# Storing the rows of each load in another order in DRAM: a decode attention and gated feed-forward kernel on one core

## The chip, the core and the metric

The kernel runs on one core of a Trainium2 chip. The metric is the device time of one execution in microseconds (us); the median of several runs is used. Beside the times there is one profiled execution, whose page and trace are read below.

## What is computed

One token is decoded for a batch of two (B = 2, D = 512). The input is normalised, and the result is the input plus an attention branch plus a feed-forward branch, all in float32. The attention has 32 heads of width 128, each with its own keys and values, and looks only at the last W = 2048 of 8192 cached positions.

```
W = min(4096, max(256, Sk // 4))              # 2048
q = (x @ wq) ... (B, Hq, Sq, Dh)
k = k_cache[:, :, Sk - W:, :]
v = v_cache[:, :, Sk - W:, :]
scores = einsum("bhqd,bhkd->bhqk", q, k) * Dh ** -0.5
o = einsum("bhqk,bhkd->bhqd", softmax(scores), v)
A = o ... @ wo
B = ((x w_gate) * (x w_up)) @ w_down          # F = 1376
out = x + A(layernorm(x)) + B(layernorm(x))
```

The caches and weights that must be read once come to 159.48 MB, and each byte is used for very little arithmetic.

## The kernel before

**One stream.** The host packs everything that the kernel reads in bulk into one flat array, `stream`, in the order of use (`laid_out`, from L495). `blocks` (L41) lists the pieces: a small first piece (normalisation input, selection matrices and the first head's weights), then steps that hold in turn keys (`k`), query weights (`wq`), values (`v`), output weights (`wo`), the feed-forward weights (`wg`, `wu`, `wd`). A piece is a block of 128 rows; row p holds what goes to SBUF partition p, and all rows of a block have one length. A full step has 13,824 floats (55,296 bytes) a row, 6,912 KB in all; 16 of the 29 stream loads are of this size. The last, shorter loads split the end of the stream, so that work on the last head can start early. One more array, `wd_rest`, holds the last 96 rows of `w_down` and is loaded as 96 rows of 512 floats, after the last stream load.

**Loads.** `pump` (L138) issues the loads from SyncE's queue (SP), one `dma_start` for each block. Full steps live in a pool `steps` of three buffers (`BUFS = 3`, L119). When a buffer's last field has been used, `done` (L164) frees it and calls `pump`, so the next load is queued behind those that are running. Nothing else issues bulk loads. A load's rows are source rows of equal length that lie one behind the other:

```
src = stream[at : at + P * (c1 - c0)].rearrange("(p i) -> p i", p=P)
sp.dma_start(tiles[key][:, c0:c1], src)
```

Both sides of this load count 128 rows, the partition being the outermost count. The hardware deals the rows of each load to 16 DMA engines.

**Compute.** For each head VectorE multiplies the keys with the broadcast query (`products`) and adds up over the head width (`sums`), GpSimd finds the maximum and the sum over the partitions, ScalarE takes the exponential (`weights`), and TensorE weighs the values (`weigh`), brings the result into place (`transpose`) and adds the output projection to one accumulator (`project_o`). The values of a head come three heads after its keys (`LAG = 3`). The class `InOrder` keeps every engine's instructions in the order in which the code writes them; since its one line L92 makes the calls, nearly all instructions stand under L92 in the profile, and groups are told apart by their tiles (`step`, `q`, `s`, `o_ps`, `acc`).

## Time and profile before

| what | value |
|---|---|
| median of 3 runs | 378.63 us (378.44 to 378.70) |
| the profiled execution's own time | 379.42 us |
| its span, first to last instruction | 377.6 us |
| read from DRAM | 159.48 MB, 422 GB/s over the span |
| busy: TensorE, VectorE, ScalarE, GpSimd | 258.7, 293.7, 58.5, 25.4 us |
| packets of the load queue, share of 16 engines | 98.2% |
| granted TensorE clock, mean | 0.783 |
| a 6,912 KB load, issue to landing, median | 33.8 us |

The span is what the page's shares refer to; the rest of the execution's time lies around it. "DMA share" is the mean busy share of the 16 DMA engines in a stretch, and GB/s is what they moved. The time from issue to landing contains the wait behind loads that are already queued. The trace also holds a record of each DMA packet, with queue, start, duration and size, but not the engine that moved it.

### The profile page before, as it was taken

To read this page: it belongs to the slowest core of one execution; us is meant where nothing else is said; L and a number is where in the kernel's file an instruction comes from. 1 tells how busy PE (TensorE), PEld (TensorE's weight loads), DVE (VectorE), ACT (ScalarE), POOL (GpSimd) and SP (SyncE) were. 2 spreads that over 40 slices of the span, in tenths; PEclk is the share of its full clock that TensorE was granted. 3 is DMA by queue.
4 is the path that set the end of the run, shared out by engine and by line. 5 is a ranking of instruction groups with operands and counts; after the bars stand their busy time and mean duration, and the time that the engine had idled before them with its cause. 6 is when DMAs were issued, how large, how long until landed. Compare 5 with 4: busy or idle time off the path is not lost.

```text
span 377.6 us, 2826 instructions
## 1 busy us (share of the span) xinstructions
PE 258.7 (69%) x1070; PEld 87.9 (23%) x1070; DVE 293.7 (78%) x144; ACT 58.5 (15%) x256; POOL 25.4 (7%) x78
## 2 busy tenths in 40 slices
PE   3386597986548586766858476585756769537995
PEld 3241122231112222212212121231211222111343
DVE  3299691998599499769949977994996799599940
ACT  1011001122011120202112020121202011211131
POOL 1001000000000001000000000000000000000010
PEclk9996968888697666868858696885968677855999
DMA  8999999899999999999999999999999999999994
GB/s 326 461 434 455 439 394 469 387 457 453 400 451 451 398 457 404 441 457 404 452 439 406 457 404 445 451 412 440 445 398 463 418 417 434 446 435 418 416 416 162
DMA packets 4328, 159.65 MB, mean 423 GB/s; under 512 B 492, under 2 KB 508, under 8 KB 988
## 3 DMA queue, kind: packets, MB, share of 16 engines
q1 hardware_dynamic: 4316, 159.48, 98.2%
q8 instruction: 8, 0.13, 0.1%
q14 instruction: 4, 0.03, 0.0%
HBM read 159.48 MB, written 0.00 MB: 422 GB/s over the span
## 4 chain that ended last, share of the span: by engine, by line
DMA 68%; PE 15%; DVE 14%; ACT 1%; SPq 1%; issue 1%; DVEq 0%
DMA step<-in_stream_dram 68%; DVE s L92 7%; DVE step L92 7%; PE o_ps L92 6%; PE q L92 4%; PE acc L92 3%; PE tr L92 1%; SPq L92 1%; ACT o_sb L92 0%; ACT oT L92 0%; DVE o_sb L92 0%; DVE m L92 0%; ACT hT L92 0%; DVE o_out L92 0%; DVE rec L92 0%
## 5 line engine op out<-in xcount | busy, mean ns | idle before, releaser
L92 DVE TENSOR_TENSOR step<-step,q 128x4096 f32<-128x4096 f32 x31 | 136.6, 4407 | 53.0 <-DMA step<-in_stream_dram 53.0
L92 PE MATMUL q<-step,xnb 128*128 128x512 f32 (+1 forms) x128 | 94.1, 886 | 74.5 <-DMA step<-in_stream_dram 74.5
L92 DVE TENSOR_REDUCE s<-step 128x32 f32<-128x4096 f32 x32 | 141.4, 4420 | 1.1
L92 PE MATMUL o_ps<-step,p 128*16 128x512 f32 x512 | 71.3, 695 | 10.6 <-DMA step<-in_stream_dram 10.6
L92 PEld LDWEIGHTS q<-step,xnb 128*128 128x128 f32 x128 | 32.9, 280 | 131.4 <-DMA step<-in_stream_dram 75.9
L92 PE MATMUL acc<-step,oT 128*17 128x512 f32 (+1 forms) x88 | 37.2, 578 | 9.3 <-ACT oT L92 8.1
L92 ACT COPY o_sb<-o_ps 128x512 f32<-128x512 f32 x24 | 14.0, 585 | 145.9 <-PE o_ps L92 145.9
L92 PE MATMUL tr<-first,o_sb 128*128 128x2 f32 (+2 forms) x192 | 26.3, 257 | 14.9 <-ACT o_sb L92 13.3
L92 PEld LDWEIGHTS tr<-first,o_sb 128*128 128x128 f32 x192 | 24.5, 196 | 36.5 <-ACT o_sb L92 33.0
L290 POOL PARTITION_ALL_REDUCE mm<-m x32 | 11.3, 355 | 286.2 <-DVE rec L92 179.9
L92 PEld LDWEIGHTS o_ps<-step,p 128*16 128x16 f32 x512 | 13.8, 107 | 70.6 <-issue 56.9
L92 ACT ACTIVATE nm<-mm 128x2 f32<-128x2 f32 x32 | 6.5, 203 | 130.2 <-POOL mm L290 130.2
L92 ACT ACTIVATE p<-s,nm 128x16 f32<-128x16 f32 x64 | 19.2, 300 | 1.0
L92 ACT ACTIVATE oT<-tr,rec 128x1 f32<-128x1 f32 x64 | 12.2, 260 | 27.1 <-PE tr L92 27.1
L306 POOL PARTITION_ALL_REDUCE sum<-rs x32 | 12.7, 398 | 53.4 <-ACT p L92 53.4
L92 PE MATMUL o_ps<-step,xn 128*2 128x512 f32 (+1 forms) x48 | 13.5, 597 | 0.0
L92 DVE TENSOR_TENSOR step<-step,tr 128x4096 f32<-128x4096 f32 x1 | 4.4, 4422 | 9.8 <-DMA step<-in_stream_dram 9.8
L92 ACT ACTIVATION_READ_ACCUMULATOR p<-s,nm 128x1 f32 x64 | 12.0, 187 | 0.0
L92 PEld LDWEIGHTS acc<-step,oT 128*17 128x17 f32 x88 | 4.9, 98 | 19.6 <-ACT oT L92 11.9
L92 PE MATMUL acc<-step,hT 128*17 128x128 f32 (+2 forms) x58 | 8.0, 361 | 0.7 <-DMA step<-in_stream_dram 0.7
L92 PE MATMUL q<-xnb,mean_w 128*128 128x512 f32 (+1 forms) x16 | 7.8, 581 | 0.0
L92 DVE TENSOR_TENSOR o_out<-acc,x_nat 128x128 f32<-128x128 f32 x1 | 0.3, 292 | 9.1 <-PE acc L92 9.1
(35 smaller groups left out, 38.5 us busy)
## 6 DMA issues: line engine op xcount, KB each, us to landing
step<-in_stream_dram SPq DMA_DIRECT2D x16, 6912.0 KB, 33.8
step<-in_stream_dram SPq DMA_DIRECT2D x2, 6400.0 KB, 32.9
step<-in_stream_dram SPq DMA_DIRECT2D x1, 6784.0 KB, 46.0
step<-in_stream_dram SPq DMA_DIRECT2D x1, 6656.0 KB, 29.2
step<-in_stream_dram SPq DMA_DIRECT2D x1, 5376.0 KB, 15.7
step<-in_stream_dram SPq DMA_DIRECT2D x1, 4864.0 KB
step<-in_stream_dram SPq DMA_DIRECT2D x2, 2304.0 KB, 17.2
step<-in_stream_dram SPq DMA_DIRECT2D x1, 1280.0 KB, 14.1
```

The costliest lines, as they stand in the source:

```text
L92: made = call(*args, **kwargs)
L290: nc.gpsimd.partition_all_reduce(mm, m, P, bass_isa.ReduceOp.max)
L306: nc.gpsimd.partition_all_reduce(sum_t[h], rs, P, bass_isa.ReduceOp.add)
```

## The change

The rows of each stream block are stored in another order. With the 128 rows numbered 8 q + n (q from 0 to 15, n from 0 to 7), row 8 q + n now lies at place 16 n + q of its block. The host stores it so, and the load's source pattern undoes it: it counts 16 (q), then 8 (n), then the row's floats. The source's outermost step is one stored row, its second step 16 stored rows. The destination is the same tile as before and gets the same row in each partition. All 29 stream loads are changed in this way, the small first one included; `wd_rest`, `x_rows` and the output are not. The order of instructions on each engine stays.

```diff
@@ -26,6 +26,8 @@
 FH = [(0, 2 * FB), (2 * FB, F)]
 LAG = 3
 RB = 16
+NQ = 16
+NR = P // NQ
 M = RB * (B - 1) + 1
@@ -158,7 +160,9 @@
             if at is None:
                 sp.dma_start(tiles[key][:FR, c0:c1], wd_rest)
             else:
-                src = stream[at : at + P * (c1 - c0)].rearrange("(p i) -> p i", p=P)
+
+                src = stream[at : at + P * (c1 - c0)]
+                src = src.rearrange("(n q i) -> q n i", n=NR, q=NQ)
                 sp.dma_start(tiles[key][:, c0:c1], src)
@@ -540,9 +544,10 @@
     parts = [
-        np.concatenate([field(kind, i) for kind, i, _ in fields], axis=1).ravel()
+        np.concatenate([field(kind, i) for kind, i, _ in fields], axis=1)
         for _, fields in blocks()
     ]
+    parts = [a.reshape(NQ, NR, -1).swapaxes(0, 1).ravel() for a in parts]
```

## The prediction

> **What bounds the kernel now.** I read the page from the top: engine shares, then the 40 slices, the queues, the chain, and last the windows of the trace and its packet records.

> ```profile
> PE 258.7 (69%) x1070; PEld 87.9 (23%) x1070; DVE 293.7 (78%) x144; ACT 58.5 (15%) x256; POOL 25.4 (7%) x78
> ...
> DMA  8999999899999999999999999999999999999994
> ...
> q1 hardware_dynamic: 4316, 159.48, 98.2%
> ...
> DMA 68%; PE 15%; DVE 14%; ACT 1%; SPq 1%; issue 1%; DVEq 0%
> ```

> No compute engine is full: VectorE, the busiest, works 78% of the span. The DMA digits are 9 nearly throughout, and the packets of queue q1 fill 98.2% of the time of 16 engines. The chain puts 68% on transfers into `step`; its PE and DVE pieces are work done between two landings while the next load is already running. So the length of the kernel is the length of the stream, and what matters is how fast each of the 16 engines gets through its rows.

> The windows (columns: stretch, busy time of PE, PEld, DVE, ACT, POOL, clock, DMA share, GB/s) show the steady rate and the tail:

> ```profile
> 20.00:60.00 40.00, 29.02 (x81) 9.25 (x79) 33.67 (x16) 4.88 (x19) 2.61 (x7) 0.83 1.00 434
> 110.00:160.00 50.00, 34.16 (x130) 10.34 (x130) 42.41 (x20) 8.07 (x38) 3.71 (x10) 0.73 1.01 437
> ...
> 371.00:372.00 1.00, 0.93 (x8) 0.93 (x8) 0.00 (x0) 0.02 (x1) 0.00 (x0) 1.00 0.65 195
> ```

> In the steady part a full DMA share moves 434 to 437 GB/s. In the tail, from 371 to 372 us, a share of 0.65 moves 195 GB/s, which is 300 GB/s per full share. The packet records say why. One packet is one row of a load, as many packets of a size as the load has rows (2048 of 55,296 bytes for 16 loads of 128 rows). In the steady part a row never varies: 2,041 ns shortest, 2,044 median, 2,049 at the ninth tenth; the 11 rows over 2,070 ns each cover the time of an instruction-load packet of q8 or q14. In the tail they vary. The last load but one has 128 rows of 4,096 bytes: 159 ns at best, but up to 287 once the rows of `wd_rest` (96 rows of 2,048 bytes) have begun beside them; those take 84 ns alone and up to 176 in that stretch (one 232). A row that takes 176 instead of 84 ns has met another that wanted the same thing at the same moment. Short fixed costs explain only part: 2,048 bytes in 84 ns on 16 engines would still be 390 GB/s.

> So two facts: rows of 128-row loads run together without touching each other, and rows of the one load that is cut up differently (96 rows, six to an engine) slow others, and are slowed, to about double.

> **The change, part by part.** *Instructions.* No compute instruction, wait, buffer or byte changes. The same 29 stream issues stand at the same places of SP's queue, the same 128 rows of the same sizes go to the same partitions, and the number of packets stays. Costs at nothing: the host's reordering is outside the measured time. An issue with one more source dimension lasts between the 0.39 us of the first load and the 0.73 us of the `x_nat` issue in the SP timeline; only the first one is uncovered, so 0 to 0.3 us. I take 0: all later ones lie beside a running load.

> *Places in DRAM.* At any moment the 16 engines read other addresses. What can that give? At most what rows now lose against their shortest time, since a row cannot be said to be read-bound when 2048 of them agree within some 0.4%. Adding packets by size, the 29 stream loads take 369.8 us per engine as measured and 367.9 at the shortest of each size: a gain of at most 1.9 us, 0.3 of which is instruction loading. The loss to be had: none that a row shows.

> [...]

> *The cut among engines.* This is the part that decides. Before, source and destination both count 128 rows, outermost. After, the source counts 16, then 8, then the row; the destination still counts 128. The engines cannot be dealt the rows by one count of 128 on both sides any more. The natural cut is by the 16: engine q gets piece q, that is rows 8 q to 8 q + 7, written to eight neighbouring partitions. The trace doesn't say which engine carries which row before, but if it were that cut already, nothing would change here; if it is another, every stream load becomes what only `wd_rest` is now: a load cut into runs of neighbouring partitions. Bounds for a row of such a load: 1.0 times its time (as the rows of 128-row loads) and 2.1 times (176 over 84). The nearest row is that of `wd_rest`, because it is the only load of this trace that isn't counted by 128 on both sides, and the slowed rows appear exactly with it. I take 2: two engines want one place and each gets half of it.

> [...]

> Would two engines that start together stay together? While they share, both run at half; when the one ahead moves on, both run at full until the other follows. Both always run at one rate, so a lead is kept and neither grows nor shrinks. The first rows of 16 engines begin within about 0.15 us, so a lead is about 0.1 us. It is saved once per change of place. I take two changes per load (a choice), so 2 x 29 x 0.1 = 5.8 us. All 16 engines must end a load before its semaphore is full, and three buffers let a luckier pair run ahead by two loads at most, so the pair with the smallest lead sets the time.

> *Sum.* Packets of queue q1 take 370.7 us per engine; the profiled execution took 379.42, so 8.8 us is start, gaps, the work after the last landing and what lies around the span; it stays. Stream rows at their shortest, 367.9, doubled: 735.7. The 96-row load, `x_nat` and semaphore packets: 0.9. 735.7 + 0.9 + 8.8 - 5.8 = 739.6, say 740. The profiled execution lies 0.2% over the 378.63 median of the runs, less than the rounding here. What hid the transfers' neighbours stays hidden: VectorE's 293.7 us fit into 740, and a step's buffer is free (1.5 heads a load, each 4.4 us of products and 4.4 of sums, are 13 us of VectorE work) long before the next 33 us load has landed, so SP's waits end earlier, not later.

> **Rivals.** *Leads grow.* If one of two sharing engines gets 51% of the place, its lead grows by 4% of what is still shared at each of 58 stays; the shared part shrinks by 0.96 each time, and 22.7 of 58 stays are shared in sum: 367.9 x 0.39 = 144 us more, 523. At 50.5% it is 34.5 stays and 598. [...] Against: the slowed 4,096-byte rows (1.8 times) and 2,048-byte rows (2.1 times) of the tail suffer alike.

> *The change doesn't alter the cut, or the place isn't shared.* Then only addresses move, and the time is that of before, 378.6. For it: the trace shows no engine numbers, and the tail's slow rows could come from mixing two sizes. Against: 6,144- and 8,192-byte rows follow each other in the queue the same way, and their ninth tenths lie within 4% of their shortest.

> *Faster, by the read side alone.* Cut unchanged, and neighbouring reads end the loss at the start, where 43,008-byte rows take 1,650 ns on average against 1,587, and the small ones everywhere. Worth the 1.6 us that isn't instruction loading: 377.0. It decides only where the place is not shared at all, since one shared row costs more than it can save. Against: nearly all rows already stand at their shortest.

> **How the numbers follow.** About 0.2% is what a measurement of this kernel can tell from no change. Full sharing, 700 to 765 (low end: leads of 0.7 us; high end: without leads the sum is 745, with 2.1 for 2 it is 782, and 765 is about half-way): 68%. Growing leads, 400 to 700: 20%. Addresses alone with no effect: 6%; faster by the read side: 3%; slightly slower (start or issue): 3%. The forecast is 740. The range of 490 to 765 holds nearly all of the first case and two thirds of the second, some 80%. Faster 0.03, same 0.06, slower 0.91.

> **What would show it.** Right: 55,296-byte rows near 4.1 us instead of 2.04, the slices near 217 GB/s with a DMA share still 9 in every slice, landings of the 6,912 KB loads about double, VectorE's share near 40%, and the chain with far more than 68% on DMA. Growing leads would show in slices that climb from 217 towards 434 GB/s over the span. Wrong: rows still at 2,041 to 2,049 ns. Then the cut is unchanged or two engines don't disturb each other, and the step "the nearest row is that of `wd_rest`" has failed.

## The result and the profile after

The changed kernel takes 770.78 us, the median of 6 runs (765.96 to 774.64); the kernel before took 378.71 us beside it. The ratio is 2.0345, with a 95% interval of 2.0303 to 2.0388. The way and the mechanism were forecast; the time lies 4% over the 740 us of the forecast and 0.8% over the upper end of its range, 765 us. The profiled execution took 765.96 us, the shortest of the six, with a span of 764.2 us.

From the page of the changed kernel: the engines' busy shares, the slices of DMA share and of GB/s, the load queue, and the chain.

```profile
PE 265.6 (35%) x1070; PEld 89.0 (12%) x1070; DVE 294.8 (39%) x144; ACT 57.9 (8%) x256; POOL 25.4 (3%) x78
...
DMA  9999999999999999999999999999999999999997
GB/s 202 227 212 187 225 189 226 191 226 192 223 194 226 194 223 197 221 197 220 197 226 198 220 200 217 200 218 206 211 217 200 226 201 209 216 223 199 210 221 171
...
q1 hardware_dynamic: 4316, 159.48, 99.2%
...
another core or an unknown queue 55%; PE 31%; DMA 10%; ACT 2%; issue 1%; SPq 0%; DVE 0%; DVEq 0%
```

The queue moves the same number of packets and the same bytes, and its 16 engines are still busy 99.2% of the span, at half the rate: 187 to 227 GB/s in every slice but the last, 209 over the span. VectorE does the same 295 us of work, now 39% of the span. The chain names most of its waiting "another core or an unknown queue". With one core and one load queue these are probably waits for landings that the profile did not tie to a load. Even if all of them are, they and DMA make 65% of the chain, not the "far more than 68%" that the prediction gave as a sign: the pieces of TensorE's work between landings grew to 31%. That landings are what is waited for, the waits of VectorE by cause say directly (columns: us in total, times, longest us; first before, then after):

```profile
DVE step L92 <- DMA step<-in_stream_dram: 62.7, 11, 9.8
...
DVE step L94 <- DMA step<-in_stream_dram: 431.1, 22, 24.9
```

The same stretches as before, by windows (busy time of PE, PEld, DVE, ACT, POOL, clock, DMA share, GB/s), and the full-size loads from issue to landing, before and after:

```profile
110.00:160.00 50.00, 19.12 (x67) 5.70 (x66) 18.09 (x8) 4.74 (x22) 1.91 (x5) 0.67 1.02 212
...
410.00:560.00 150.00, 48.50 (x172) 14.99 (x171) 64.72 (x31) 11.95 (x58) 6.04 (x16) 0.64 1.00 209
```

```profile
step<-in_stream_dram SPq DMA_DIRECT2D x16, 6912.0 KB, 33.8
...
step<-in_stream_dram SPq DMA_DIRECT2D x16, 6912.0 KB, 85.7
```

A full DMA share moves 212 GB/s where it moved 437, and landings come 85.7 us after the issue instead of 33.8, 2.5 times where about double was forecast (this time contains the wait behind loads queued earlier). The packet records show it row by row. A 55,296-byte row had 2,044 ns as its median; now it is 4,301, the mean 4,233. Since a packet of an engine begins within some 20 ns of the end of its last one, the records can be sorted into 16 chains, 128 full-size rows in each. One such chain, in ns, sixteen rows in a row:

```
4105 4307 4301 4288   4067 4296 4304 4304   4069 4292 4301 4305   4075 4294 4298 4307
```

The rows come in groups of four: the first is a little shorter, and three take 4.30 us. A reading of this, an estimate from these rows and the forecast's two changes of place per load: of its eight rows of a load an engine writes four to one place and then four to the next, and in the short row its partner was still in the other place. The experiments test it.

### The profile page after: what moved, and what is told of

It is laid out like the page before. It is cut to its first block, busy times and chain, and to the rows that moved or that the text cites. A ratio compares the mean times of both kernels' runs of the same rounds, so it can differ in the third digit from the quotient of the medians.

```text
span 764.2 us, 2826 instructions
## 1 busy us (share of the span) xinstructions
PE 265.6 (35%) x1070; PEld 89.0 (12%) x1070; DVE 294.8 (39%) x144; ACT 57.9 (8%) x256; POOL 25.4 (3%) x78
## 2 busy tenths in 40 slices
DMA packets 4328, 159.65 MB, mean 209 GB/s; under 512 B 492, under 2 KB 508, under 8 KB 988
## 3 DMA queue, kind: packets, MB, share of 16 engines
q1 hardware_dynamic: 4316, 159.48, 99.2%
HBM read 159.48 MB, written 0.00 MB: 209 GB/s over the span
## 4 chain that ended last, share of the span: by engine, by line
another core or an unknown queue 55%; PE 31%; DMA 10%; ACT 2%; issue 1%; SPq 0%; DVE 0%; DVEq 0%
PE q L94 13%; DMA step<-in_stream_dram 10%; PE o_ps L94 10%; PE acc L94 5%; PE tr L94 3%; ACT o_sb L94 1%; ACT oT L94 1%; SPq L94 0%; DVE o_sb L94 0%; ACT hT L94 0%; DVE o_out L94 0%; ACT nm L94 0%; DVEq L94 0%
## 5 line engine op out<-in xcount | busy, mean ns | idle before, releaser
L94 PE MATMUL q<-step,xnb 128*128 128x512 f32 (+1 forms) x128 | 96.3, 904 | 401.0 <-DMA step<-in_stream_dram 401.0
L94 PE MATMUL o_ps<-step,p 128*16 128x512 f32 x512 | 75.5, 722 | 61.8 <-DMA step<-in_stream_dram 61.7
L94 PE MATMUL acc<-step,oT 128*17 128x512 f32 (+1 forms) x88 | 35.3, 553 | 9.3 <-ACT oT L94 8.7
L94 DVE RECIPROCAL rec<-sum 128x2 f32<-128x2 f32 x32 | 4.9, 155 | 8.8 <-POOL sum L310 8.8
## 6 DMA issues: line engine op xcount, KB each, us to landing
step<-in_stream_dram SPq DMA_DIRECT2D x16, 6912.0 KB, 85.7
```

What stands on the lines that cost most here:

```text
L94: made = call(*args, **kwargs)
```

## The experiments

Three theories are kept apart: **A**, the load is cut among the engines in another way, and pairs of engines then write to one place in SBUF; **B**, 16 engines that read neighbouring rows of DRAM at once disturb each other; **C**, a source with three counts is slow by itself.

### The order kept, the cut taken back

The rows still lie so that engines read neighbours, but the source counts 32 groups of four rows instead of 16 of eight.

```diff
-NQ = 16
+NQ = 32
```

> Row 4 g + r at place 32 r + g, source counted 32 x 4: engines still read neighbouring rows, source has three counts, but the slowest count (32) can be dealt in the same way as 128. Theory A (the cut into runs of eight partitions makes pairs of engines meet at one place): 55,296-byte rows back at 2.04 us, time 378 to 380 us, same as before. Theory B (reading neighbouring DRAM rows at once is slow): stays near 770 us, rows 4.2 to 4.3 us. Theory C (a source with three counts is slow by itself): near 770 us too. If neighbouring reads help at all, up to 1.6 us faster than before.

Measured: 379.64 us against 378.63 (ratio 1.0033, interval 1.0017 to 1.0048). Windows and full-size loads of this kernel:

```profile
110.00:160.00 50.00, 33.97 (x130) 10.42 (x130) 43.00 (x20) 8.12 (x38) 3.38 (x9) 0.76 1.02 439
```

```profile
step<-in_stream_dram SPq DMA_DIRECT2D x16, 6912.0 KB, 33.7
```

439 GB/s and 33.7 us: the stream is that of before, and the median full-size row is back at 2,044 ns. Neighbouring reads and three counts cost nothing like 390 us, so C is out as its cause, and B as far as these reads are neighbours. That 32 is dealt as 128 is, is told from these row times; no record names the engine. Nothing was gained from the read side either, as its ceiling of 1.9 us in the forecast allowed for.

### The cut kept, the order taken back

The rows lie in the order of before; a gap of 16 floats after every eight rows keeps the counts 16 and 8 apart.

```diff
+GAP = 16
...
-                src = stream[at : at + P * (c1 - c0)]
-                src = src.rearrange("(n q i) -> q n i", n=NR, q=NQ)
+                src = stream[at : at + P * (c1 - c0) + NQ * GAP]
+                src = src.rearrange("(q m) -> q m", q=NQ)[:, : NR * (c1 - c0)]
+                src = src.rearrange("q (n i) -> q n i", n=NR)
...
```

> Rows in the order of before, but counted 16 x 8 with a gap of 64 bytes after every eight rows, so that the two counts stay apart. Engines read rows that lie eight rows from each other, as far apart as the change's reason supposed for before. Theory A (cut): near 770 us (765 to 785), rows 4.2 to 4.32 us. Theory B (neighbouring reads): 379 to 381 us. Theory C (three counts): near 770 us. If the part of a slowed row above twice 2,041 ns comes from neighbouring reads, rows at most 4.1 us and some 750 us.

Measured: 770.17 us, ratio 2.0344 (2.0309 to 2.0378), the changed kernel's own figure. The windows:

```profile
110.00:160.00 50.00, 18.22 (x50) 5.62 (x50) 18.09 (x8) 4.59 (x21) 1.91 (x5) 0.63 1.03 211
```

Its full-size rows take 4,325 ns at the median, the changed kernel's 4,301. With the run above this separates the two halves of the edit and leaves B no room: the order of the rows carries none of the loss, the count 16 x 8 carries all of it, and what a row takes beyond double is not caused by neighbouring reads.

### Which partitions share a place

Small loads were put ahead of the kernel before, to see which rows slow each other. The first two attempts said little. In the first, two-row loads ran while the other engines had already gone on to the next loads:

> Before, with seven small loads of two rows ahead (two engines, one partition each, a size of its own for each load), to see which two partitions share a place. Partitions 32 apart (27,392 bytes) and 1 apart (26,368): both rows about 2.1 times their lone time, 2.0 to 2.15 us and 1.95 to 2.07 us. 64 apart (27,136), 16 apart (26,880), 36 apart (26,624), 8 apart (26,112), 96 apart (25,856): lone time, 0.96 to 1.02 us. A place that follows the partition number in blocks of eight would give 1 apart slow and 32 apart fast; no sharing at all gives all seven near 1 us.

Partitions 0 and 32 took 1.76 and 1.81 us against 1.01 lone, and 0 and 1 took 1.52 and 1.55 against 0.98: slowed, but less than the 2.0 to 2.15 and 1.95 to 2.07 expected. And 1 and 65 took 1.52 and 1.35, 4 and 12 took 1.74 and 1.32, and the second row of 5 and 101 took 1.81, where none was expected to be slow; only the pairs 16 and 36 apart stayed near their lone time. That doesn't fit by itself; an engine of another load may have stood at the same place. So each load was made to wait for the one before it:

> Before, with twelve small loads ahead, one row to an engine, each waiting for the one before, so that no other load runs beside them; each has its own row size s. Lone time is s / 27.07 + 2 ns (1.48 to 1.58 us). Theory A (a place is four neighbouring partitions together with the four that lie 32 above): pairs 0 and 32 (42,752 bytes), 0 and 1 (42,496) about 2.1 times the lone time; 0 and 64 (42,240), 0 and 16 (41,984), 0 and 36 (41,728), 0 and 4 (41,472), 0 and 96 (41,216) the lone time; partitions 0 to 3 on four engines (40,960) 4 times or a little more; twelve rows nine partitions apart (40,704) lone time; sixteen rows 8, 4 or 2 apart (40,448, 40,192, 39,936) 2.1 times. If the part above 2 belongs to the shared place, the pair 0 and 32 already shows it; if it belongs to all 16 engines running at once, the pairs show 2.0 and the sixteen rows 2.1. If read order or load form mattered, 0 and 64 would be as slow as 0 and 32.

One row to an engine mixes the sharing with what a first row takes longer (in the third attempt, below, first rows of two-engine loads that don't meet took 1,735 to 2,773 ns, their later rows 1,552 to 1,571). Partitions 0 to 3 on four engines took 4.32 to 4.58 us, 2.9 to 3.0 times the lone time where 4 was expected, and twelve rows nine apart 1.78 to 1.97, 1.2 to 1.3 times. The loads of sixteen rows took 1.5 to 2.1 times, where 2.1 was expected. But pairs overlapped: 0 and 32 took 1.57 to 1.59 times and 0 and 1 took 1.72, while 0 and 96, which should be lone, took 1.53 to 1.57, and 0 and 64, 0 and 36, 0 and 4 up to 1.46. Only the extremes are told apart, and the numbers expected were missed. The third attempt gave each engine several rows, so that the later rows could be read:

```diff
+    GROUPS = [(8, 2, 4), (9, 2, 4), (1, 2, 4), (16, 2, 4), (1, 2, 2), (8, 4, 4), (1, 8, 4), (1, 16, 4), (2, 16, 4)]
+    for j, (gap, k, m) in enumerate(GROUPS):
+        n = 10752 - 64 * (j + 1)
+        src = stream[: k * m * n].rearrange("(m k i) -> k m i", k=k, m=m)
+        sp.dma_start(tiles["s", 0][: gap * (k * m - 1) + 1 : gap, :n], src)
...
```

> Before, with nine small loads ahead, each alone on the queue, several rows to an engine, the rows told apart by size. Written as partitions of engine 0, engine 1 and so on. Theory A, a place is four neighbouring partitions and the four that lie 32 above; lone time s / 27.07 + 2 ns, a first row up to 0.6 us longer, later rows as follows. 42,752 bytes: 0, 8, 16, 24 against 32, 40, 48, 56, which meet row by row: 2.0 to 2.12 times. 42,496: 0, 9, 18, 27 against 36, 45, 54, 63, which don't: 1.0. 42,240: 0-3 against 4-7: 1.0. 41,984: 0, 16, 32, 48 against 64, 80, 96, 112: 1.0. 41,728: 0, 1 against 2, 3: 2.0 to 2.12. 41,472: four engines, in steps of 8 over 0 to 120: 2.0 to 2.12. 41,216: eight engines with four neighbours each, 0 to 31: 1.0. 40,960: sixteen with four neighbours each, 0 to 63: 2.0 to 2.12. 40,704: sixteen, every second partition, 0 to 126 (the change's cut): 2.0 to 2.12. If the part above 2 belongs to the place, the two-engine loads show it; if to 16 engines at once, only the last two. Without places, all nine alike.

From the packet records (lone: the time expected of a row alone):

```
engines and partitions                    lone ns   rows, ns
 2: 0 8 16 24 | 32 40 48 56               1581      2394 to 3118
 2: 0 9 18 27 | 36 45 54 63               1572      first 2434, 2564; all later 1571
 2: 0-3 | 4-7                             1562      first 1992, 2773; all later 1561
 2: 0 16 32 48 | 64 80 96 112             1553      first 1735, 2465; all later 1552
 2: 0 1 | 2 3                             1543      3105 to 3206
 4: steps of 8, 0 to 120                  1534      2378 to 3148
 8: four each, 0-31                       1525      first up to 2388; median 1524
16: four each, 0-63                       1515      median 3204, 2.115 times
16: every second partition, 0-126         1506      median 3090, 2.05 times
```

### The lead between partners

Two loads ahead of the changed kernel give some engines extra rows, so that partners are out of step.

```diff
+    LEAD = 4
...
+    for k, p0, gap in ((12, 32, 4 // LEAD), (4, 80, 12 // LEAD)):
+        src = stream[: k * LEAD * STEP].rearrange("(m k i) -> k m i", m=LEAD, k=k)
+        sp.dma_start(tiles["s", 2][p0 : p0 + gap * (k * LEAD - 1) + 1 : gap, :], src)
...
```

> The change, with two extra loads ahead of all others into a buffer that is overwritten later: one gives four rows of 55,296 bytes to each of 12 engines, the next four rows to each of 4 of them. If these are engines 0-11 and 0-3, engines 0-3 lag 4-7 by four rows, and 8-11 lag 12-15 by four rows (8.2 us each), so that partners are always at different places. Theory A with leads that are kept: 379 + 16 us of extra loads + some 20 us where the rows are shorter than the lead: 395 to 430 us, 55,296-byte rows mostly at 2.04 us. Theory A with leads that do not last: 600 to 790 us. Theories B and C: 770 + 16 = 787 us.

Measured: 594.44 us (590.16 and 598.71), which no theory had forecast (two runs): the lead helps greatly, as A alone allows, but the full effect (395 to 430) didn't come. Windows of this run:

```profile
100.00:200.00 100.00, 54.02 (x212) 17.11 (x210) 58.11 (x28) 12.82 (x59) 5.29 (x14) 0.74 1.01 329
200.00:300.00 100.00, 51.57 (x184) 15.62 (x184) 59.62 (x26) 9.92 (x46) 4.53 (x12) 0.64 1.00 321
...
400.00:450.00 50.00, 23.10 (x82) 7.22 (x82) 27.19 (x12) 4.90 (x23) 2.27 (x6) 0.65 0.99 250
450.00:500.00 50.00, 18.14 (x72) 5.48 (x72) 27.01 (x11) 3.39 (x14) 1.51 (x4) 0.66 0.98 251
```

Same loads, same cut, same reads as in the changed kernel, but 321 to 329 GB/s instead of 209 to 212, because the engines are out of step. From 82 to 103 us one chain reads, in ns, 3911 2578 2104 2073, 3818 2458 2085 2069: of four rows one is shared, one in part, two are nearly free. The lead wasn't the planned one from the start: the extra rows themselves met others (4.1 to 4.3 us each in part), and the third buffer, which they fill, could be loaded only after they had landed:

```profile
3.13 33.47 SPq L94 DMA_DIRECT2D step<-in_stream_dram  x3
```

That line of SP's timeline holds the wait. When it ended, at 36.6 us, the packet records have four engines at their first row of 43,008 bytes, eight at their sixth and four one row into the load after it: with the partners that the run assumes, leads of about five and of three rows, where four was planned for all. By theory A a lead that isn't four rows leaves part of each group of four shared. What took part of the lead away between 300 and 350 us is open. The same with two rows:

> As the run with the four-row lead, with two rows instead of four to the 12 and to the 4 engines. There the steady stretch ran at 322 to 329 GB/s until 300 us, and 240 to 250 after it; rows came in groups of four with one long, one half-long and two lone ones. Theory A with kept leads: about half of that effect, 255 to 275 GB/s in the stretch from 100 to 250 us and a total of 630 to 720 us, with rows in groups of four of which about one is near 2.1 to 2.6 us and three are long. Leads without effect: 208 to 212 GB/s and 770 to 785 us.

Measured: 752 us (747.78 and 756.28); 630 to 720 was expected, and the forecast of half the effect failed. Windows:

```profile
110.00:160.00 50.00, 30.26 (x94) 9.56 (x94) 27.03 (x11) 4.95 (x21) 1.51 (x4) 0.74 0.99 215
410.00:560.00 150.00, 41.18 (x164) 13.16 (x164) 59.13 (x28) 10.70 (x51) 5.29 (x14) 0.63 0.99 224
```

Here the planned lead was mostly gone early, and where it went is open: at 117 us a chain reads 3502 4342 4338 4189, 3476 4334 4340 4186 ns, so a group of four saves about 1 us, not 4. But this small lead stays, group after group, and is somewhat larger 370 us later (2.9 us for the shortest row of a group). So in this run a lead lasted for some 370 us, though it drifted; setting one of a chosen size by extra loads is what failed.

### The price per load

Every second one of the 16 full-size loads in the new order, all others as before.

```diff
+def moved(key):
+    return key[0] == "s" and 3 <= key[1] <= 17 and key[1] % 2 == 1
...
```

> The change in 8 of the 16 full-size loads only, every second one of the steps 3 to 17; all other loads as before. Theory A, price per load: a changed load takes 8 x (4,233 - 2,047) ns = 17.5 us more, so 378.6 + 8 x 17.5 = 518.5 us, and somewhat more where an engine that is still in a load of one cut meets one in a load of the other: 515 to 545 us. If the slowdown were a state that the whole queue falls into, nearer to 770; if the loads hid behind each other, nearer to 379.

Measured: four runs took 537.2, 538.3, 573.2 and 575.8 us; the ratio of 1.4189 (1.416 to 1.4218) is that of the two shorter ones, and the profile is of the longest. For most of that profile the loads alternate cleanly: eight rows such as 3902 4325 4309 4326 4146 4316 4328 4326, then 2580 and seven of 2042 to 2049 ns. So the loss is paid load by load, and is over with the next load but for its first row or two (the first takes up to 3.6 us later on). A state of the whole queue, near 770, and loads that hide behind each other, near 379, are both refuted.

The 19 us above 518.5 in the two shorter runs lie inside what was expected for meetings of the two cuts (515 to 545); the two longer runs lie outside. In the one that was profiled some rows between 427 and 466 us took 5.2 to 6.7 us, up to 3.3 times 2,041 ns, a few engines fell behind, and from 485 to 510 us the others had nothing left to do: the mean DMA share was 0.15. That three engines were at one place there, where the two cuts met, is argued from the length of the rows and not shown. No profile shows the 19 us of the shorter runs.

### The third count by itself

The order-kept run was 0.3% slower than before. The same count of 32 x 4 with the order of before (gap after every four rows) asks which of the two costs that.

> Rows in the order of before, counted 32 x 4, with a gap of 64 bytes after every four rows: three counts as in the run with neighbouring reads and 32 x 4, the reads as far apart as before. That run took 379.64 us against 378.63, ratio 1.0033. If its 1 us comes from the third count (a first issue of 0.65 instead of 0.39 us, and the like), this one takes 379.2 to 380 us as well; if it comes from neighbouring reads, 378.5 to 378.8 us. Either way rows of 55,296 bytes near 2.04 us.

Measured: 379.43 us, ratio 1.0022 (1.0011 to 1.0033), beside 1.0033 (1.0017 to 1.0048) with neighbouring reads. So there is a cost without neighbouring reads; a rest for them isn't shown, as the intervals overlap. A part is seen at the start. SP's timeline of the kernel before, and of this one:

```profile
0.72 0.39 SPq L92 DMA_DIRECT2D first<-in_stream_dram  x1
1.18 1.35 SPq L92 DMA_DIRECT2D step<-in_stream_dram  x3
```

```profile
0.72 0.66 SPq L95 DMA_DIRECT2D first<-in_stream_dram  x1
1.44 1.87 SPq L95 DMA_DIRECT2D step<-in_stream_dram  x3
```

The first issue lasts 0.27 us longer, which is uncovered; later issues lie beside running loads. No run of this study has a median below that of the kernel before.

## Why the prediction was right in kind and short in size

**What bounds the kernel.** Right. The stream set the time before and sets it after; 2.1 times the row time made 2.03 times the kernel time.

**Instructions.** The issue was put at 0 out of 0 to 0.3 us; it is 0.27 us in the changed kernel as well, too little to matter here.

**Places in DRAM.** Right: at most 1.9 us to be gained, none found. Two readings of the packet records are slightly off: of the 11 rows over 2,070 ns, 10 cover an instruction-load packet and the one of 2,088 ns doesn't; and two 4,096-byte rows of the tail took 344 and 384 ns, more than the 287 named.

**The cut.** Right, though only one short stretch of the tail spoke for it (rows of 84 ns that took up to 176); that pieces of eight rows would meet in pairs was the author's estimate, shown by no row then. The two halves of the edit and the runs with small loads now show it. Which engine has which partitions is still not on record; the groups of four rows, and the small load that gave sixteen engines every second partition (2.05 times), fit the cut forecast. With that cut, and since 64 shares with neither 0 (1,552 ns, alone 1,553) nor, with it, 32, the pairs would be engines 0 to 3 with 4 to 7, and 8 to 11 with 12 to 15: an estimate from the runs with small loads.

**The price of a shared row.** This is the step that failed: "I take 2: two engines want one place and each gets half of it." A row that is shared all the way takes 4,301 to 4,319 ns (the median and the ninth tenth of all full-size rows), 2.11 times 2,041. The rows at hand had said up to 2.1 (176 over 84; the records have 175), and the prediction had written that down as the upper bound and then chosen the round figure. That those rows gave just this figure was partly luck: the 4,096-byte rows beside them gave 1.8, one row of 84 ns took 232, and in the profiles of the two 32 x 4 runs such rows took up to 225 and 234. On 367.9 us of rows at their shortest, 2.107 (4,301 over 2,041) instead of 2 is 39 us. The part above 2 belongs to the shared place rather than to reads: old order and new order show it alike, and it is there in the lone load of sixteen engines over 64 partitions (2.115). Why it is more than 2 is not known. Two engines alone at one place took 3,105 to 3,206 over 1,543 ns, 2.01 to 2.08 times; the two later rows, free of the start, took 3,188 and 3,206. So part of it is there without the other fourteen.

**The leads.** Right that they last, wrong in size. Stream rows in the profiled run sum to 756.7 us per engine, some 18.5 less than all of them would at 2.107 times. Put down to leads, this remainder is 0.32 us for each of 2 x 29 stays, where 0.1 was taken. In the full-size loads alone it is 0.27, and there the short row of a group shows it directly: about 4.05 instead of 4.30 us. The rows of the small first load took 91 ns at the median before and after, so they hardly shared; this was not followed up. The two changes of place per load, a choice then, are the groups of four in the chains.

**The sum.** 739.6, plus 39.4 for the price, less 12.7 for the larger leads (that remainder less the 5.8 taken), and less 0.4 in the rest (8.0 us around the packets for 8.8 foreseen, 0.4 more in small packets) is 765.9, the profiled execution's 765.96. It comes out because the leads are what was left over; what it shows is that two terms were mis-sized and partly cancel. The other runs lie up to 774.64; the leads that a run begins with may differ, but no profile of those runs was read.

**The range.** 765 was put half-way between the sum without leads at a factor of 2 (745) and at 2.1 (782). At the factor that the tail had shown, the measured 770.8 would have been inside, as 782 is the upper end then.

**The rivals.** Leads that grow: hardly seen, and far too slow to matter (the shortest row of a group goes from 4.1 to 3.9 us in some 500 us). Addresses alone: refuted by the 770.78 us itself, and by the 770 us of the old order with the 16 x 8 count. Faster by the read side: with the new order and the cut of before the time was 379.64 us, not below 378.63.

## What to carry to other kernels

Here a source counted 16 x 8 made a row take 4,301 ns instead of 2,044, although destination, sizes and instructions stayed the same, and one counted 32 x 4 left it at 2,044; the reading is that 16 x 8 changed which DMA engine writes which partition. Look at the outermost count on both sides of a load before looking at addresses. Where the rows before all took one time (2,041 ns shortest, 2,049 at the ninth tenth) and the load queue's packets filled 98.2% of the engines' time, another order in DRAM had at most 1.9 us to gain and gained none, and engines that met all the time cost a factor of 2.1 a row. When the nearest rows of a trace give factors of 1.8 to 2.1, let the range run to the sums at both of them, rather than to a round figure from an argument.

## What the runs showed of the hardware that was not expected

Two engines at one place get less than it gives to one: two rows of 55,296 bytes in 4,301 ns are 25.7 GB/s, one alone in 2,041 ns is 27.1 GB/s. A count of 32 x 4 in the source leaves the rows at 2,044 ns, a count of 16 x 8 does not, so it isn't the number of counts that decides. And engines out of step stayed out of step for a while: the same cut ran at 209 to 212 GB/s with partners in step and at 321 to 329 GB/s for some 200 us with leads of a few rows. In the run with half of the full-size loads changed, some rows took 6.1 to 6.7 us, three times their shortest and more.
